# A list scheduler that waits longer for urgent work: up to 1.2 lengths of an operation instead of 0.5, in the front of a transformer block

## The chip, the cores and the metric

The kernel runs on one core of a Trainium2 chip. The metric is the device time of one execution in microseconds (us). Executions of one kernel agree within about 0.3%. All runs here were with a granted TensorE clock of 0.999 or 1.000. The profile's "span", from first to last instruction, is 1.7 to 1.8 us shorter than the time of the same execution. Engines: PE is TensorE (PEld its weight loads), DVE is VectorE, ACT is ScalarE, POOL is GpSimd, SP is the engine that issues most transfers.

## The reference

A pre-normalised block: linear attention with 32 heads and the feature map `phi`, then a gated feed-forward part, each added to its input. Sequence 2048, width 1024, inner width 3584, bf16 inputs.

```python
def _A_ref(x, wqkv, wo):                      # linear attention
    q, k, v = split_heads(x @ wqkv)           # cut
    pq, pk = phi(q), phi(k)                   # t + 1 for t > 0, else exp(t); + 1e-6
    kv = einsum("bhsd,bhse->bhde", pk, v);  z = sum of pk over s
    o = (pq @ kv) / (pq @ z + 1e-6)
    return merge_heads(o) @ wo
def _B_ref(x, W_gate, W_up, W_down):
    gate = x @ W_gate;  up = x @ W_up
    return (relu(gate) * up) @ W_down
h   = x + _A_ref(layernorm(x), wqkv, wo)
out = h + _B_ref(layernorm(h), W_gate, W_up, W_down)
```

## The kernel before

The large products use a seven-product scheme: sums and differences of blocks are formed on VectorE ("sums" in what follows), seven products are taken in place of eight, and their outputs are combined. The kernel's body does not issue instructions. It hands them to a `Plan`, which records what each reads and writes, gives each a length by a formula, and then fixes the order on every engine by simulating one schedule when the kernel is built. The order is all that survives: on the chip each engine executes its list, and semaphores make it wait.

The length formulas (`hold` is how long the engine is taken, `lat` what follows until others see the result, `acc` a surcharge for an accumulated output, `psum` whether an input lies in PSUM):

```python
if eng == "vector":
    narrow = all(self.nbytes(a) == 2 and a.space != PSUM for a in (out, *ins) if self.free(a) > 1)
    mode = {"tensor_tensor": 2, "tensor_scalar": 4, "memset": 2}.get(op, 1) if narrow else 1
    ...                                                    # cut
    return n / (0.96 * mode) + 69 + acc, 95 + self.SEM
if eng == "scalar":
    return n / 1.2 + (51 if psum else 93) + 2 * acc, 105 + self.SEM
return n * 1.15 + 100, 60 + self.SEM                       # GpSimd
```

The choice at each step (`late` is the time by which an operation should start if TensorE is not to wait, `ready` when its inputs are there, `s` the plan's clock on this engine, `a` the candidates whose predecessors are placed):

```python
now = [i for i in a if nodes[i].ready <= s]
i = min(now, key=lambda i: (nodes[i].nom if e == "tensor" else nodes[i].late, i))
v = nodes[i]
if e != "tensor":
    soon = [j for j in a if s < nodes[j].ready < s + 0.5 * v.hold and nodes[j].late < v.late - 1500.0]
    if soon:                                   # let the engine idle for the more urgent one
        i = min(soon, key=lambda j: (nodes[j].late, j))
        v = nodes[i]
        s = v.ready
v.start = s
clock[e] = s + v.hold
```

`Tile_.norm` applies the second normalisation to a tile on GpSimd, reading and writing 1024 bf16 elements per partition; a transposing transfer follows and feeds the gate stage. `Norm.finish` does the same for most tiles of the first normalisation; those are the GpSimd steps before 80 us.

Of the kernel before, what the change touches and what calls it, by code (L numbers as in the profile page):

```python
# [32 lines left out]
class Plan:  # L33
# [6 lines left out]
    WINDOW = 6000.0  # L40
    AHEAD = 120000.0
    OPENING = 45000.0

    class Node:
        __slots__ = ("eng", "calls", "preds", "hold", "lat", "open", "dma", "late", "ready", "left", "start", "nom")
# [155 lines left out]
    def schedule(self):  # L201
        nodes = self.nodes
        succs = self.order()
        engines = ("tensor", "vector", "scalar", "gpsimd", "sync")
        avail = {e: [] for e in engines}
        clock = {e: 0.0 for e in engines}
        for i, v in enumerate(nodes):
            v.left, v.ready = len(v.preds), max(0.0, v.late - self.AHEAD) if v.dma else 0.0
            if v.eng != "tensor" and v.late > 2.0 * self.OPENING:

                v.ready = max(v.ready, self.OPENING)
            if not v.left:
                avail[v.eng].append(i)
        pe = [i for i, v in enumerate(nodes) if v.eng == "tensor"]
        done, first, wire, out = set(), 0, 0.0, []
        while True:
            best = None
            for e in engines:
                a = avail[e]
                if not a:  # L220
                    continue
                if e == "sync":
                    for i in a:
                        v = nodes[i]
                        if v.late - max(clock[e], v.ready) > 6000.0:
                            v.ready = max(v.ready, wire - 2000.0)
                if e == "tensor":
                    while first < len(pe) and pe[first] in done:
                        first += 1
                    limit = nodes[pe[first]].nom + self.WINDOW  # L230
                    a = [i for i in a if nodes[i].nom <= limit]
                    if not a:
                        continue
                s = max(clock[e], min(nodes[i].ready for i in a))
                if best is None or s < best[0]:
                    best = (s, e, a)
            if best is None:
                break
            s, e, a = best
            now = [i for i in a if nodes[i].ready <= s]  # L240
            i = min(now, key=lambda i: (nodes[i].nom if e == "tensor" else nodes[i].late, i))
            v = nodes[i]
            if e != "tensor":

                soon = [j for j in a if s < nodes[j].ready < s + 0.5 * v.hold and nodes[j].late < v.late - 1500.0]
                if soon:
                    i = min(soon, key=lambda j: (nodes[j].late, j))
                    v = nodes[i]
# [3 lines that stand above are left out]
            end = s + v.hold + v.lat  # L252
            if v.dma:
                wire = max(wire, s + v.hold) + v.dma
                end = wire + v.lat - v.dma + min(4000.0, max(0.0, 0.25 * (v.late - s)))
            elif e == "sync":

                end = max(end, min(wire + 800.0, end + 2500.0))
            avail[e].remove(i)
            done.add(i)  # L260
            out.append(i)
            for j in succs[i]:
                w = nodes[j]
                r = clock[e] if w.eng == e else end
                w.ready = max(w.ready, r)
                w.left -= 1
                if not w.left:
                    avail[w.eng].append(j)
        assert len(out) == len(nodes)
        self.span = max(clock.values())  # L270
        return out
# [1303 lines left out]
```

## Time and profile before

| kernel before | us |
|---|---|
| median of 3 runs (lowest, highest) | 727.81 (727.63, 728.01) |
| span of the profiled execution | 724.3 |
| TensorE busy | 714.4 |
| stalls between matmuls, whole kernel | 10.2 |

The last row is what the distance between two matmul starts has over the usual one (215.9, 109.2 or 57.5 ns after 512, 256 or 132 columns; the prediction says why). Some profiles lack matmul records, but none lacks weight-load records, and each weight load starts 1 to 2 ns after the matmul before it. In the experiments I therefore took the starts from the weight loads and the widths from the program.

```profile
L122 DVE TENSOR_TENSOR mem<-mem 128x1024 f16<-128x1024 bf16 x10 | 6.8, 692 | 0.0
```

### The profile page before, as it was taken

What the parts mean: (1) busy time and instruction counts of PE and PEld (TensorE: products, weight loads), DVE (VectorE), ACT (ScalarE), POOL (GpSimd) and SP (SyncE); (2) the same over time, 40 slices, a digit from 0 to 9 for tenths busy, and PEclk for the clock granted to TensorE, in tenths of its full rate; (3) what the DMA queues carried; (4) which work ended last, traced back from release to release, by engine and by line L of the source; (5) the groups of instructions that cost most, each with busy time, mean ns of one, the idle gap of its engine ahead of it and who ended that gap; (6) DMA issues with size and microseconds to landing.
All of it is one profiled execution on the core that took longest, in us unless ns stands there. A gap on an engine that the chain in (4) does not pass through costs nothing.

```text
span 724.3 us, 11221 instructions
## 1 busy us (share of the span) xinstructions
PE 714.4 (99%) x4163; PEld 396.7 (55%) x4163; DVE 563.9 (78%) x954; ACT 277.3 (38%) x540; POOL 77.8 (11%) x88
## 2 busy tenths in 40 slices
PE   8999999999999999999999999999999999999998
PEld 4444545444444444444444444444444688888887
DVE  7897745887796885666767968769758879899996
ACT  5877555666554443333333333333333220001100
POOL 1342000002202110000000000000000004001452
PEclk9999999999999999999999999999999999999999
DMA  9556406069766630446145575685681878777974
GB/s 300 165 117 110 138 0 212 23 109 216 160 156 151 140 73 6 129 136 186 60 139 188 165 244 157 202 253 186 198 262 51 276 265 209 216 265 238 242 80 60
DMA packets 156503, 117.40 MB, mean 162 GB/s; under 512 B 54944, under 2 KB 140192, under 8 KB 156320
## 3 DMA queue, kind: packets, MB, share of 16 engines
q1 hardware_dynamic: 148832, 113.01, 53.9%
q0 software_dynamic: 7616, 3.67, 4.8%
q8 instruction: 32, 0.52, 0.3%
q14 instruction: 23, 0.19, 0.1%
HBM read 70.52 MB, written 34.08 MB: 144 GB/s over the span
## 4 chain that ended last, share of the span: by engine, by line
PE 85%; DVE 2%; DMA 2%; ACT 1%; issue 0%; POOL 0%; ACTq 0%
PE psum L122 85%; DVE mem L122 2%; DMA mem<-mem 2%; ACT mem L122 1%; POOL mem L122 0%; ACT tiny L122 0%; DVE tiny L122 0%; ACTq L122 0%
## 5 line engine op out<-in xcount | busy, mean ns | idle before, releaser
L122 PE MATMUL psum<-mem 128*128 128x512 f16 (+4 forms) x4147 | 713.3, 334 | 6.5 <-ACT mem L122 2.7
L122 PEld LDWEIGHTS <-mem 128*128 128x128 f16 (+1 forms) x4163 | 396.7, 98 | 323.8 <-issue 8.0
L122 DVE TENSOR_TENSOR mem<-psum,mem 128x512 f32<-128x512 f32 (+2 forms) x240 | 187.4, 794 | 99.3 <-ACT mem L122 65.1
L122 DVE TENSOR_TENSOR mem<-mem 128x512 f16<-128x512 bf16 (+8 forms) x400 | 241.6, 643 | 14.9 <-DMA mem<-mem 9.6
L122 ACT COPY mem<-psum 128x512 f32<-128x512 f32 (+2 forms) x124 | 92.7, 749 | 209.4 <-PE psum L122 197.9
L122 ACT COPY psum<-psum 128x512 f32<-128x512 f32 (+1 forms) x68 | 49.1, 722 | 160.3 <-PE psum L122 147.6
L122 POOL DMA_DIRECT2D out_dram<-mem x28 | 34.1, 1299 | 413.8 <-DVE mem L122 413.7
L122 ACT ACTIVATE mem<-psum 128x512 bf16<-128x512 f32 x90 | 53.6, 598 | 18.5 <-PE psum L122 18.0
L122 DVE SCALAR_TENSOR_TENSOR mem<-mem 128x512 bf16<-128x512 bf16 (+1 forms) x71 | 57.7, 813 | 1.3
L122 POOL TENSOR_SCALAR mem<-mem,tiny 128x1024 bf16<-128x1024 bf16 x28 | 37.5, 1338 | 196.9 <-ACT tiny L122 176.8
L122 DVE SCALAR_TENSOR_TENSOR mem<-psum,mem 128x512 bf16<-128x512 f32 x66 | 45.4, 688 | 11.9 <-PE psum L122 7.9
L122 ACT ACTIVATE mem<-mem,tiny 128x1024 bf16<-128x1024 bf16 x24 | 27.4, 1143 | 11.0 <-DVE tiny L122 5.8
L122 DVE TENSOR_SCALAR mem<-mem 128x512 bf16<-128x512 bf16 (+1 forms) x49 | 16.3, 332 | 17.6 <-ACT mem L122 17.4
L122 DVE TENSOR_TENSOR mem<-psum,tiny 128x384 bf16<-128x384 f32 (+1 forms) x48 | 22.9, 508 | 5.3 <-ACT tiny L122 3.9
L122 ACT ACTIVATE mem<-mem 128x1024 bf16<-128x1024 f32 (+1 forms) x23 | 24.3, 1056 | 6.5 <-DVE mem L122 6.4
L122 ACT ACTIVATE tiny<-tiny 128x1 f32<-128x1 f32 (+2 forms) x112 | 22.8, 206 | 7.5 <-DVE tiny L122 4.7
L122 ACT ACTIVATE tiny<-psum 128x12 f32<-128x12 f32 (+1 forms) x48 | 8.1, 169 | 13.9 <-PE psum L122 13.4
L122 DVE BATCH_NORM_STATS2 tiny<-mem 128x6 f32<-128x512 bf16 x16 | 10.2, 682 | 2.5 <-DMA mem<-in_A_x_dram 2.5
L122 ACT CAST mem<-psum 128x512 bf16<-128x512 f32 x18 | 10.4, 582 | 4.2 <-PE psum L122 3.7
L122 POOL TENSOR_SCALAR tiny<-tiny 128x1 f32<-128x1 f32 x14 | 4.7, 337 | 25.2 <-ACT mem L122 13.3
L122 ACT ACTIVATION_READ_ACCUMULATOR mem<-mem,tiny 128x1 f32 x24 | 4.5, 188 | 0.0
L122 DVE TENSOR_SCALAR tiny<-tiny 128x1 f32<-128x1 f32 x16 | 3.4, 210 | 0.3
(18 smaller groups left out, 14.4 us busy)
## 6 DMA issues: line engine op xcount, KB each, us to landing
l_dram<-mem SPq DMA_DIRECT2D x98, 128.0 KB, 2.2
mem<-l_dram SPq DMA_DIRECT2D x12, 896.0 KB, 6.4
mem<-in_A_x_dram SPq DMA_DIRECT2D x32, 256.0 KB, 3.0
mem<-in_B_W_up_dram SPq DMA_DIRECT2D x14, 512.0 KB, 5.3
mem<-in_B_W_gate_dram SPq DMA_DIRECT2D x14, 512.0 KB, 4.3
mem<-in_B_W_down_dram SPq DMA_DIRECT2D x28, 256.0 KB, 3.4
r_dram<-mem SPq DMA_DIRECT2D x56, 128.0 KB, 1.8
mem<-r_dram SPq DMA_DIRECT2D x8, 896.0 KB, 5.0
```

Source lines behind the costliest of these rows:

```text
L122: call = lambda: getattr(getattr(self.nc, eng), op)(*args, **k)
```

## The change

Its intent: while the plan's clock is below 215 us, that is up to the gate and up stage, an engine may idle for up to 1.2 lengths of the operation that it would otherwise start, if a more urgent one becomes ready in that time.

```diff
+    SHORT = 215000.0
...
-                soon = [j for j in a if s < nodes[j].ready < s + 0.5 * v.hold and nodes[j].late < v.late - 1500.0]
+                wait = (1.2 if s < self.SHORT else 0.5) * v.hold
+                soon = [j for j in a if s < nodes[j].ready < s + wait and nodes[j].late < v.late - 1500.0]
```

## The prediction

> **What bounds the kernel now.** I read the page first for engine totals, then busy time in stretches, then the chain that ended last, then what TensorE waited for, and last the timeline around its largest stalls.
>
> ```profile
> span 724.3 us, 11221 instructions
> PE 714.4 (99%) x4163; PEld 396.7 (55%) x4163; DVE 563.9 (78%) x954; ACT 277.3 (38%) x540; POOL 77.8 (11%) x88
> ```
>
> TensorE is busy for 714.4 of 724.3 us, at full granted clock, so all idle time it has is 9.9 us. The busy share alone does not prove it well fed, because a record of 379 ns covers a matmul that starts every 216 ns. I therefore also took the starts of consecutive matmuls from the trace. In the dense stretches a 512-column matmul follows the last after 215.9 ns, a 256-column one after 109 ns, a 132-column one after 57.5 ns. Whatever a gap has beyond that is a stall.
>
> The stretches show where stalls lie (columns: stretch; its length, then busy us and instructions of each engine):
>
> ```profile
> 0.00:45.00 45.00, 42.49 (x209) 19.51 (x210) 35.47 (x65) 32.16 (x71) 13.16 (x32) 1.00 0.74 207
> 45.00:100.00 55.00, 54.22 (x297) 26.24 (x296) 40.98 (x76) 36.41 (x70) 10.72 (x13) 1.00 0.45 104
> 100.00:215.00 115.00, 111.83 (x616) 54.48 (x615) 87.77 (x181) 66.36 (x167) 10.07 (x8) 1.00 0.58 136
> 215.00:400.00 185.00, 185.00 (x883) 84.94 (x882) 129.60 (x229) 70.15 (x136) 9.81 (x8) 1.00 0.45 120
> ...
> 660.00:725.00 65.00, 60.82 (x558) 54.27 (x555) 57.25 (x75) 4.97 (x9) 24.23 (x20) 1.00 0.68 140
> ```
>
> From 215 us on TensorE is full until the tail, which is the last matmul's drain, a DVE add and a store, and has nothing to do with the order of the front. The chain says the same in one line, start and length first:
>
> ```profile
> 208.32 512.51 PE psum L122 x3082
> ```
>
> So only the first 208 us can be shortened. Its stalls by my gap count after 12 us (before that it is start-up loads) are: 0.70 us at 27.8, 0.12 and 0.22 at 41, 0.73 at 54.1, 0.25 and 0.23 at 68, 0.22 at 76, 0.31 at 127.6, 0.21 and 0.18 at 146, 0.94 and 0.03 at 150, 1.62 at 191.1, 0.72 at 201.7, and 0.28, 0.09 and 0.23 at 205 to 208. Sum **7.1 us**. That is the ceiling of any gain: 1.0% of 727.8. What TensorE's stalls are put down to (total us, times, longest):
>
> ```profile
> PE psum L122 <- ACT mem L122: 2.7, 3, 1.5
> PE psum L122 <- DVE mem L122: 1.1, 2, 0.6
> PE psum L122 <- DMA mem<-mem: 0.8, 1, 0.8
> ```
>
> These sums are below 7.1 because the records of the last matmul before a gap run on into it. The largest stall has this timeline (start, length, instruction):
>
> ```profile
> 189.60 1.06 ACT L122 ACTIVATE mem<-mem 128x1024 bf16<-128x1024 f32 x1 [1.15 <-DVE mem L122]
> 190.56 1.14 ACT L122 ACTIVATE mem<-mem,tiny 128x1024 bf16<-128x1024 bf16 x1
> 191.60 0.19 ACT L122 ACTIVATION_READ_ACCUMULATOR mem<-mem,tiny 128x1 f32 x1
> 191.69 0.58 ACT L122 ACTIVATE mem<-psum 128x512 bf16<-128x512 f32 x1
> 192.17 0.57 ACT L122 COPY mem<-psum 128x512 f32<-128x512 f32 x1
> 192.63 0.59 ACT L122 COPY psum<-psum 128x512 f32<-128x512 f32 x1
> 192.79 1.46 PE L122 MATMUL psum<-mem 128*128 128x512 bf16 x6 [1.46 <-ACT mem L122]
> ```
>
> ScalarE began a square of the second normalisation (1.14 us and 0.19 for its accumulator) at 190.56. The copy of a product bank that TensorE needs next became ready at about 191.28 (the matmul at 190.90 plus its 0.38) and started only at 192.17, behind square and exp. This is the picture that the change wants to avoid: a long, patient operation starts just before a short, urgent one is ready.
>
> **What the Trainium skill says.** "PSUM — Partial Sum Buffer", section "Engine vs sequencer instructions", says that the queues of ScalarE, VectorE and GpSimd are strictly first in, first out, and that matmuls start and complete in program order. The trace agrees: the copy at 192.17 was ready and still stood behind the square. So the order that the plan emits is the order that the chip keeps, and a wrong hold is paid in full. "Perfetto Trace Analysis", section "Identifying the Most-Contended Engine", warns that matmul busy share is no measure of distance to the roofline and proposes the share of weight loads. Here that share is 55%, because one 98 ns load goes with each 216 ns matmul and, from 600 us on, with each 109 ns one; in this kernel the spacing of starts says more. The same page, section "Optimization Strategy", says to take the gaps of the critical engine and see what releases them; that is the list above.
>
> **The change, part by part.** No instruction is added or removed: the same 11,221 go out in another order. The plan is a list scheduler run when the kernel is built. When an engine has a ready operation v, it looks whether an operation with a deadline at least 1.5 us earlier becomes ready soon; if so, the engine idles until then and takes that first. "Soon" was 0.5 of v's planned length, and is now 1.2 of it while the plan's clock is under 215 us; later it stays 0.5. The plan's lengths, by its own cost lines: a ScalarE square of 1024 with accumulator 1024/1.2+93+170 = 1116 ns, so it waits up to 1.34 us where it waited 0.56; a 1024-wide exp from memory 946 ns (1.14 for 0.47); a VectorE 1024-wide f32 join 1136 ns (1.36 for 0.57); a bn_stats half or a 512-wide join 602 ns (0.72 for 0.30). The trace has 1146, 1056, 1223 and about 685 ns for them, so the plan is 3 to 14% short. The test also covers GpSimd and the DMA queue, not only the two engines named.
>
> How many could be affected: in the first 208 us ScalarE has 16 squares, 15 wide exps and 8 wide copies with accumulator, and VectorE 15 wide joins and 12 wide form sums; 66 long operations, each a place where the rule may fire. Short ones gain too little reach (0.1 to 0.2 us) to matter.
>
> What it can save: the stalls that stand behind such an operation. At 191.1 nearly all, 1.62 less the 0.57 us copy that TensorE must await but had partly hidden: about 1.2. At 27.8 two bn_stats halves stand before an add that TensorE needs: up to 0.7. At 201.7 a VectorE queue of join and sums precedes what TensorE awaits: perhaps 0.4. At 54.1 the copy starts as soon as its matmul group is done, so there is nothing to save, and the 0.94 at 150 waits for a transpose DMA. The dozen small ones: say 0.5 of their 2. Sum **about 2.8 us** if all fall out well.
>
> What it costs: each hold idles its engine for up to 1.3 us where it would have worked. Off the critical path this is free as long as there is slack, and there is: over 0 to 215 us VectorE is busy 164.2 of 215 us (76%), ScalarE 134.9 (63%). But the delayed square or statistics feed a normalisation, a transpose DMA and then the next stage's left sums; that chain already binds just ahead of the gate stage (around 180 to 208 us the chain is ACT, POOL, DMA, DVE by turns). I put off 0.6 us for one or two such new stalls. Net about **-2.2 us**, that is 725.6.
>
> **The rivals.** First, a wash: the plan's clock and the chip's differ by fractions of a us, so that the operation that the plan holds for is ready earlier or later on the chip. For it speaks that at 190.56 the exp's bank had been finished at about 190.42 on the chip already, so the plan's order there came from its deadlines or its own clock, and a longer hold need not touch it. Result 727 to 728.5. Second, the new order makes a longer stall: the holds delay norms, the transposes come late, and the gate stage starts later than 208 us. For it speaks the 0.94 us stall on a transpose at 150 and the thin margin in 180 to 208; against it the 24 to 37% slack. Result 728.5 to 731. Third, the holds gain almost everything, because order changes propagate and clear the 201 to 208 group as well: 721 to 723. The DMA or another engine becoming the bound is excluded: the bytes are the same, and the matmul stream from 208 us on is gapless for 512 us.
>
> **Range and chances.** I weigh the main path (-1 to -3.5 us) at 0.58, the wash at 0.22, the worse order at 0.12, the large gain at 0.08. Middle 725.6, eight in ten between 722.4 and 728.9. Faster by 2% needs 14.6 us, twice the 7.1 us that exist: 0.005. Slower by 2% needs 14.6 us of new stalls in 208 us of work: 0.015. Within 2%: 0.98.
>
> **What would show it.** Right: the long piece of TensorE work at the end of the chain keeps its length (512.5 us) and starts earlier, at about 206 instead of 208.3; the 1.62 us stall near 191 falls below 0.6; the stall near 27.8 shrinks; ScalarE shows more small idle pieces ahead of copies from PSUM, and busy totals stay. Wrong in size: the gap list after 12 us still sums to about 7, with other places. Wrong in sign: TensorE waits for transposes or for VectorE sums between 140 and 208 us, and the long piece starts after 209. Wrong in kind: any new gap after 215 us, where the rule did not change but inherits the state of a shifted plan; that would mean that order changes leak into the gate stage.

## More of the kernel before

Besides the views in the prediction two more are needed. One is the 1024-wide sums of the front, as a group (count, busy us, mean ns of one). The other is VectorE on the timeline ahead of the largest stall (start, length, instruction, and in brackets how long the engine idled before it and what ended that):

```profile
187.93 0.42 DVE L122 TENSOR_TENSOR mem<-mem 128x512 f16<-128x512 bf16 x1 [2.76 <-DMA mem<-mem]
188.27 0.68 DVE L122 SCALAR_TENSOR_TENSOR mem<-psum,mem 128x512 bf16<-128x512 f32 x1
188.88 0.08 DVE L122 DVE_READ_ACCUMULATOR mem<-psum,mem 128x1 f32 x1
188.88 0.69 DVE L122 TENSOR_TENSOR mem<-psum,mem 128x512 f32<-128x512 f32 x1
```

A sum sits at the head of VectorE's queue and waits 2.76 us for a transposing transfer. Behind it stand a join and an add that read finished products.

`GW.sums` forms four differences of gate and up weights for each group; they are needed only when the gate stage starts, so in the plan they have 47 to 56 us of slack.

## The result, and the profile after

| | median us | lowest to highest | runs |
|---|---|---|---|
| before | 727.72 | 726.88 to 728.07 | 6 |
| changed | 727.68 | 727.52 to 728.00 | 6 |

The ratio is 1.0002 (95% interval 0.9989 to 1.0015). Ratios here are the mean time of one kernel's fast runs over that of the other's in the same rounds, so not quite the ratio of the medians quoted. The change did nothing that can be measured.

The head of the changed kernel's page:

```profile
span 725.8 us, 11170 instructions
...
PE 711.1 (98%) x4112; PEld 396.6 (55%) x4163; DVE 566.4 (78%) x954; ACT 276.9 (38%) x540; POOL 80.4 (11%) x88
```

The program still has 4163 matmuls; 51 of their records are missing, as the count of weight loads shows, and with them 3 us of "busy". The busy time in stretches:

```profile
45.00:100.00 55.00, 52.77 (x287) 25.95 (x292) 41.69 (x79) 36.97 (x74) 13.99 (x15) 1.00 0.49 115
100.00:215.00 115.00, 111.66 (x601) 54.30 (x611) 89.46 (x179) 67.05 (x168) 9.87 (x8) 1.00 0.57 134
215.00:400.00 185.00, 184.16 (x872) 85.09 (x887) 129.36 (x232) 70.31 (x136) 9.82 (x8) 1.00 0.46 121
```

The 0.84 us that TensorE seems to idle in 215 to 400 are missing records (887 weight loads, 872 matmuls); by the weight loads there is no stall. In 45 to 100 us GpSimd is busy for 13.99 us where it was 10.72. What TensorE's stalls are put down to:

```profile
PE psum L123 <- DVE mem L123: 3.1, 5, 1.5
PE psum L123 <- ACT mem L123: 2.8, 3, 1.9
PE psum L123 <- DMA mem<-mem: 0.6, 1, 0.6
```

Waits for VectorE grew from 1.1 to 3.1 us; those for ScalarE stayed. So the change did not find nothing to do. It removed stalls and made others. A place-by-place account follows, in us. It has two profiles of each kernel, because the first profile of before was a fast execution (726.09) and the second (727.37) is nearer to the median; times in the heading are those of the first profile of before.

| stalls of TensorE | before | before, again | changed | changed, again |
|---|---|---|---|---|
| start, under 12 | 2.85 | 3.35 | 3.12 | 4.12 |
| 28 | 0.70 | 0.68 | 1.64 | 1.52 |
| 40 to 52 | 0.36 | 0.36 | 0.02 | 0.02 |
| 54 | 0.73 | 1.61 | 2.08 | 2.08 |
| 60 to 100 | 0.76 | 0.98 | 0.18 | 0.18 |
| 125 to 156 | 1.77 | 1.78 | 1.29 | 1.31 |
| 160 to 185 | 0.02 | 0.02 | 1.23 | 1.24 |
| 191 | 1.62 | 1.30 | 0.37 | 0.37 |
| 195 to 215 | 1.37 | 1.37 | 1.68 | 1.68 |
| sum | 10.2 | 11.4 | 11.6 | 12.5 |
| span | 724.3 | 725.6 | 725.8 | 726.7 |

Against the second profile of before, the first of the changed kernel gains 0.34 + 0.80 + 0.49 + 0.93 = 2.6 us at four places and loses 0.96 + 0.47 + 1.21 + 0.31 = 3.0 us at four others. The start varies by itself.

The loss at 160 to 185 has a shape of its own: three stalls, of 0.21, 0.50 and 0.51 us, at 166, 171 and 176. The second, on the timeline of VectorE, of GpSimd and of TensorE:

```profile
169.29 1.19 POOL L123 TENSOR_SCALAR mem<-mem,tiny 128x1024 bf16<-128x1024 bf16 x1 [4.09 <-ACT tiny L123]
...
169.87 1.15 DVE L123 TENSOR_TENSOR mem<-mem 128x1024 f16<-128x1024 bf16 x1
...
170.94 0.68 DVE L123 SCALAR_TENSOR_TENSOR mem<-psum,mem 128x512 bf16<-128x512 f32 x1
...
171.68 1.02 PE L123 MATMUL psum<-mem 128*128 128x512 bf16 x4 [0.34 <-DVE mem L123]
```

A 1024-wide sum takes 1.15 us, begins inside a GpSimd step and ends 0.54 us after it; the join behind it, for which TensorE waits, is late. As a group the sums now read

```profile
L123 DVE TENSOR_TENSOR mem<-mem 128x1024 f16<-128x1024 bf16 x8 | 6.9, 858 | 0.1
```

and the mean rose from 692 to 858 ns because three of the eight take 1.15 us and five 0.68. Those three are `GW.sums`, and in the kernel before they ran at 137.6, 138.3 and 143.7 us. In the changed plan the longer hold passed them over again and again: something more urgent was always due within 0.72 us (1.2 of their planned 0.602). They came to run at 164.6, 169.9 and 175.2.

The Trainium skill has the mechanism. "SBUF — State Buffer", section "Who interferes with whom", says that VectorE and GpSimd share one pair of ports to the memory under an exclusive lock, that "A DVE instruction with two SBUF inputs contends with a GpSimd instruction that reads SBUF", and that the loser blocks until the other is through. The trace agrees: in all three cases the sum ends 0.54 or 0.55 us after the GpSimd step.

The gain at 191 is on VectorE too. The same place in the changed kernel:

```profile
188.51 0.69 DVE L123 SCALAR_TENSOR_TENSOR mem<-psum,mem 128x512 bf16<-128x512 f32 x1 [0.36 <-PE psum L123]
...
189.37 0.69 DVE L123 TENSOR_TENSOR mem<-psum,mem 128x512 f32<-128x512 f32 x1
189.98 1.54 DVE L123 TENSOR_TENSOR mem<-mem 128x512 f16<-128x512 bf16 x4
```

Join and add now come first, and the sum that waits for the transfer comes after them. In the plan the join was due 0.18 us after the sum; half of the sum's planned length of 0.336 us is 0.168, so the old rule missed it by some 0.01 us, and 1.2 lengths caught it. ScalarE's order around 191 (copy, wide exp, square, exp, copy) is the same in both kernels.

The largest stall of the changed kernel, 2.08 us at 54, shows the same meeting from GpSimd's side (ScalarE, GpSimd and TensorE):

```profile
50.06 4.38 POOL L123 TENSOR_SCALAR mem<-mem,tiny 128x1024 bf16<-128x1024 bf16 x2
...
54.65 1.15 ACT L123 ACTIVATE mem<-mem,tiny 128x1024 bf16<-128x1024 bf16 x1 [1.94 <-POOL tiny L123]
...
57.23 1.02 PE L123 MATMUL psum<-mem 128*128 128x512 f16 x4 [1.92 <-ACT mem L123]
```

The two GpSimd steps take 2.53 and 1.85 us, where others take 1.19; four of VectorE's two-input sums run beside them. ScalarE has a square at the head of its queue that waits 1.94 us for GpSimd, and behind it stand the copies that TensorE needs. This is read from the trace; no run tested it alone.

### The profile page after: what moved, and what is told of

It is laid out like the page before. It is cut to its first block, busy times and chain, and to the rows that moved or that the text cites. A ratio compares the mean times of both kernels' runs of the same rounds, so it can differ in the third digit from the quotient of the medians.

```text
span 725.8 us, 11170 instructions
## 1 busy us (share of the span) xinstructions
PE 711.1 (98%) x4112; PEld 396.6 (55%) x4163; DVE 566.4 (78%) x954; ACT 276.9 (38%) x540; POOL 80.4 (11%) x88
## 4 chain that ended last, share of the span: by engine, by line
PE 88%; ACT 2%; DMA 1%; issue 1%; DVE 1%; POOL 0%; DVEq 0%; ACTq 0%
PE psum L123 88%; ACT mem L123 1%; DVE mem L123 1%; DMA mem<-in_B_W_up_dram 1%; DMA mem<-mem 0%; ACT tiny L123 0%; DVE tiny L123 0%; POOL tiny L123 0%; DVEq L123 0%; ACTq L123 0%
## 5 line engine op out<-in xcount | busy, mean ns | idle before, releaser
L123 PE MATMUL psum<-mem 128*128 128x512 bf16 (+4 forms) x4096 | 710.0, 334 | 11.1 <-DVE mem L123 3.1
L123 POOL TENSOR_SCALAR mem<-mem,tiny 128x1024 bf16<-128x1024 bf16 x28 | 39.7, 1417 | 182.3 <-ACT tiny L123 168.9
L123 DVE SCALAR_TENSOR_TENSOR mem<-psum,mem 128x512 bf16<-128x512 f32 x66 | 45.2, 687 | 10.2 <-PE psum L123 6.3
```

What stands on the lines that cost most here:

```text
L123: call = lambda: getattr(getattr(self.nc, eng), op)(*args, **k)
```

## The experiments

Theory: the gains and the losses are both real, and the largest loss comes from sums that the hold pushed beside GpSimd's steps. Rivals: (a) elastic: the chain of normalisations sets when the product near 191 may start, so any stall before it is only moved; (b) run-to-run timing of transfers decides; (c) a full VectorE queue, not GpSimd, makes the stalls at 166 to 176.

Medians of before were 727.27, 727.44 and 727.63 us (9 runs each). All results were correct. Edits are against the changed kernel's line `wait = ...` unless said.

**The two kernels again.** No edit.

> The kernel before, unchanged, for a second profile. If TensorE's stalls follow from the order (theory), the list after 12 us repeats: 7.1 to 7.5 us in sum, with 1.62 near 191, 0.70 near 27.8 and 0.73 near 54.1, each within 0.1. If run-to-run timing of transfers decides (rival), single stalls differ by 0.5 us or more and the span lies up to 1.7 us above the 724.3 of the first profile.

> The changed kernel, unchanged, for a second profile. Theory of cancelling: the same stalls again, about 1.6 at 28, 2.1 at 55, 0.2 + 0.5 + 0.5 at 166, 171 and 176, 0.4 at 193.5, sum 8.5; ratio 0.999 to 1.001. Rival (run-to-run timing): the stalls at 28 and 55 move by 0.5 us or more between the two profiles.

Before: 727.38 us, 0.9999 (0.9985 to 1.0013). Changed: 727.97, 1.0004 (0.9990 to 1.0017). The table above has the stalls. Most repeat within 0.1 us. In before those at 54 (0.73 and 1.61), at 191 (1.62 and 1.30) and at 76 (0.22 and 0.44) do not, nor does the start; the first two were expected to. In both profiles of before one 512-wide sum just ahead of the stall at 54 begins 0.17 us after the record of a GpSimd step. In the faster one the sum took 0.42 us and GpSimd's step 1.48; in the slower the sum took 1.30 and the step 1.19. In four of the five profiles with the order of before up to there, the stall is 1.61. Rival (b) holds for the start and for 54, for a third of a microsecond at 191, and not for the rest.

**The far sums stay where they were.** "Far" means more than 35 us of slack; over such an operation the old 0.5 stays.

```diff
+wait = (1.2 if s < self.SHORT and v.late - s < 35000.0 else 0.5) * v.hold
```

> The longer hold, except over operations with more than 35 us of slack, so the gate weights' sums stay near 138 to 155 us. Theory: the three sums take 0.69 us instead of 1.15, the stalls at 166, 171 and 176 (1.22 us in sum) go, and TensorE passes 192 us and the span ends 1.2 us earlier than in the changed kernel, ratio about 0.998 against before. Rival (elastic): the chain of normalisations sets the start of the product near 193 anyway, the wait there grows by 1.2 us and the span stays as in the changed kernel.

726.98 us, 0.9995 (0.9983 to 1.0008); span 725.2. The four sums run at 139.9 to 157.2 us and take 0.68 each, and the stalls at 160 to 185 are 0.02 in sum. At 191 the stall is 0.37 as in the changed kernel, so nothing was moved there: against (a). 0.78 us came back at 125 to 156, so the net against the changed kernel is about 0.6 us by the span and 1.0 by the medians, less than the 1.2 expected.

**One engine alone.**

```diff
+wait = (1.2 if s < self.SHORT and e == 'vector' else 0.5) * v.hold    # VectorE alone
+wait = (1.2 if s < self.SHORT and e == 'scalar' else 0.5) * v.hold    # ScalarE alone
```

> The longer hold for VectorE alone. If ScalarE's holds caused the longer stall at 55 us (they postpone a square that then stands behind a late GpSimd step), that stall is back at 0.7 us and the span is 1.3 us shorter than the changed kernel's; the 166 to 176 stalls stay at 1.2. If VectorE's holds caused it by slowing GpSimd, it stays at about 2. The 1.62 us stall of before at 191 stays gone if VectorE's hold over the sum that waits for the transpose removed it, and comes back if ScalarE's hold over the square did.

> Longer hold for ScalarE alone. Theory: no stalls at 166 to 176 (the sums stay), the 191 stall stays at 1.3 to 1.6 because VectorE's order there is as before, and the stall at 55 is 1.4 to 2.1, as long as in the changed kernel; ratio 1.000 to 1.002. If ScalarE's holds are what gains (as predicted), the 191 stall falls below 0.6 here and the ratio is under 0.999.

VectorE alone: 726.48 us, 0.9987 (0.9974 to 0.9999). The 191 stall is gone (0.00), those at 166 to 176 are there (1.23), the places around 54 sum to 1.07 (neither the 0.7 nor the 2 of the expectation), and 195 to 215 costs 2.07 where before had 1.37. ScalarE alone: 726.75 us, 0.9990 (0.9978 to 1.0003), where 1.000 to 1.002 was expected. The 191 stall is 1.44, no stalls at 160 to 185 (0.02), 54 at 1.44; it gains at 60 to 100 (0.08). So VectorE's holds cured 191 and made 166 to 176. The prediction had given 191 to ScalarE.

**VectorE alone, far sums stay; and both engines from 100 us on, far sums stay.**

```diff
+wait = (1.2 if s < self.SHORT and e == 'vector' and v.late - s < 35000.0 else 0.5) * v.hold
+wait = (1.2 if 100000.0 <= s < self.SHORT and v.late - s < 35000.0 else 0.5) * v.hold
```

> Longer hold for VectorE alone and never over operations with more than 35 us of slack. Theory (gains are real, losses are the collisions of VectorE with GpSimd): the 166, 171 and 176 stalls (1.22 us) of the VectorE-only version go, the rest stays; span 1.2 us under that version, ratio about 0.997 against before. Rival (elastic): the time stays at the VectorE-only version's 0.9987.

> Longer hold for both engines only from 100 us of the plan on, and never over operations with more than 35 us of slack. Theory: up to 100 us the order is that of before, so stalls to there are as in the two profiles of before (1.0 in 12 to 45, 1.5 to 2.6 in 45 to 100); none at 166 to 176; 191 at 0.4 instead of 1.3 to 1.6; span about 1.0 us under before, ratio 0.998 to 0.999.

The first: 726.77 us, 0.9990 (0.9976 to 1.0003), not the 0.997 expected. The 166 to 176 stalls went (0.02), but 125 to 156 cost 1.79 instead of 1.02, 191 0.57 instead of 0.00, and in the profiled execution 54 cost 2.00 instead of 1.07. The second: 727.43, 0.9996 (0.9984 to 1.0009). Its stalls came as expected (0.02 at 160 to 185, 0.37 at 191), but 195 to 215 cost 0.32 more than before and 125 to 156 0.3 more, so of 0.93 gained at 191 some 0.3 is left, and the timed runs do not show even that.

**Only the sums moved, into and out of GpSimd's way.** Both are the kernel before, with a line ahead of the scheduling loop that makes these operations ready no earlier than a given time. The first uses the 0.88 us slots that overlap a GpSimd step, as the changed plan did; the second uses 1.45 us slots of the same stage in which GpSimd rests.

```diff
+for i, at in ((545, 166400.0), (548, 171450.0), (554, 176500.0)): nodes[i].ready = at
+for i, at in ((545, 163950.0), (548, 169000.0), (554, 174050.0), (557, 179100.0)): nodes[i].ready = at
```

> The kernel before with one thing altered: three of the gate weights' sums may not start before 166.4, 171.45 and 176.5 us of the plan, as in the changed kernel, where each has a slot of 0.88 us beside a GpSimd step. Theory (shared access to memory): they take about 1.15 us instead of 0.69, end some 0.55 us after GpSimd's step, and TensorE loses 0.2 + 0.5 + 0.5 us near 166, 171 and 176. Rival (elastic): the same stalls, but the one at 191 shrinks by as much.

> As the last, but the sums are put in the same busy stage at 163.95, 169.0, 174.05 and 179.1 us of the plan, where GpSimd rests. Theory: they take 0.69 us each and TensorE loses nothing there (under 0.1). Rival (a full VectorE queue, not GpSimd, makes the stalls): stalls of 0.2 to 0.5 us at three of these places too.

Beside GpSimd: 729.47 us, 1.0026 (1.0012 to 1.0040), slower than before beyond the noise. The three sums take 1.15 us, TensorE loses 0.22, 0.51 and 0.51 us at 167, 172 and 177, and the stall at 191 did not shrink but grew to 2.08. The fourth sum followed by itself, to 173.9 us, clear of GpSimd, and took 0.68. Clear of GpSimd: 727.38 us, 0.9997 (0.9983 to 1.0011), sums of 0.68 us, no stall over 0.04 at 160 to 185, 191 at 1.35. That settles (a). Against (c) speaks that the lost time lies inside the sum's own record (1.15 instead of 0.68); but the slots of the two runs also differ in width, so the second run alone does not exclude a fuller queue. The timeline with the sums beside GpSimd:

```profile
165.23 1.20 POOL L122 TENSOR_SCALAR mem<-mem,tiny 128x1024 bf16<-128x1024 bf16 x1 [3.33 <-ACT tiny L122]
...
165.81 1.15 DVE L122 TENSOR_TENSOR mem<-mem 128x1024 f16<-128x1024 bf16 x1
...
166.89 0.68 DVE L122 SCALAR_TENSOR_TENSOR mem<-psum,mem 128x512 bf16<-128x512 f32 x1
```

and clear of it:

```profile
164.36 1.20 POOL L122 TENSOR_SCALAR mem<-mem,tiny 128x1024 bf16<-128x1024 bf16 x1 [3.33 <-ACT tiny L122]
...
167.22 0.68 DVE L122 TENSOR_TENSOR mem<-mem 128x1024 f16<-128x1024 bf16 x1
...
167.82 0.69 DVE L122 TENSOR_TENSOR mem<-psum,mem 128x512 f32<-128x512 f32 x1
```

The reader is to compare the 1024-wide sum of each: the same instruction type, in the same stage, 0.47 us longer where the GpSimd step covers its start.

**A plan that knows of the shared access.** A flag marks VectorE sums with both inputs in memory and GpSimd steps of 512 elements or more. A flagged operation starts no earlier than the end of the other engine's last flagged one, and VectorE prefers other ready work meanwhile.

```diff
+held = {"vector": 0.0, "gpsimd": 0.0}
...
+if e == "vector" and s < held["gpsimd"]:
+    now = [i for i in now if not nodes[i].pair] or now
...
+if v.pair:
+    s = max(s, held["vector" if e == "gpsimd" else "gpsimd"])
+    held[e] = s + v.hold
```

It was run with three hold rules: that of before (0.5); 1.2 for both engines with far sums staying; 1.2 for VectorE alone with far sums staying.

> The order rule of before (0.5), but the plan knows that VectorE's two-input sums and GpSimd steps never run side by side. Theory of two gains: the stall at 55 is under 0.5 us in place of 0.7 to 1.6, the 191 stall stays at 1.3 to 1.6; ratio about 0.9985. If this knowledge alone made the best version, it gets 0.997.

> The longer hold for both engines, not over operations with more than 35 us of slack, with the same knowledge of GpSimd. Theory: the 28 and 55 stalls fall below 1.1 and 0.5 us, 166 to 176 none, 191 at 0.4; ratio 0.996 to 0.998. If ScalarE's holds harm by themselves, the stall at 55 stays over 1.4 us and the ratio is 0.998 to 1.000.

> As the VectorE-only version without far operations, and the plan also knows that a VectorE operation with two inputs in memory and a GpSimd operation never run side by side, and lets VectorE take other work meanwhile. Theory: VectorE's two-input sums that overlap GpSimd fall from about ten in the changed kernel to two or less, their mean is under 0.02 us above the undisturbed one, and the stalls at 28 and 55 fall below 1.0 each; ratio 0.996 to 0.998. Rival: the plan's clock is too far off to avoid them, and it equals the version without this knowledge.

With the rule of before: 727.25 us, 0.9998 (0.9985 to 1.0012); the stall at 54 stays at 1.61, so what I expected of the knowledge alone did not come. With both engines: 726.90, 0.9992 (0.9979 to 1.0004); 54 at 2.05, which is the branch of the expectation in which ScalarE's holds harm. With VectorE alone: **725.32 us** against 727.44, 0.9970 (0.9957 to 0.9982), the largest gain (VectorE alone, at 0.9974 to 0.9999, is only just clear of before); 160 to 185 at 0.02, 191 at 0.37, and 54 at 0.24. Its five runs (724.69 to 725.63) all lie below the five of the version without the knowledge (726.39 to 727.85). Of its gain the cure at 191 is understood. Why 54 clears with this combination and not with either half is not: I saw it in one profile. There the two GpSimd steps at 52.9 and 54.8 us take 1.19 us each and no square waits for GpSimd; but ten of VectorE's two-input sums of the front still lie beside a GpSimd step, not two as expected; two of them are lengthened, by 0.9 us together, and the stall at 28 is 1.06. The plan's clock differs from the chip's by up to 4.0 us in the front (the product at 165.0 us was planned for 168.5 in before), so a plan can only make such meetings less likely.

## Why the prediction was right or wrong

- **The bound and the ceiling** were right. From 208 us on TensorE had nothing to gain; past the last stall of the front, at 211.7, the lag between the two first profiles stays at 1.43 us to the end. No new stall appeared after 215. The rule could only move the front's 7 us of stalls, and 2% was out of reach.
- **The time** was inside the range, 2.1 us above the point, but that is owed to the range's width: the main path, -1 to -3.5 us, missed, and the time fell where the rival of a wash had put it. The step that failed is "Net about **-2.2 us**". Its cost of "0.6 us for one or two such new stalls" was mis-sized: the losses measured 3.0 us. Its gain of 2.8 was about right in sum (2.6 measured), but by luck, since it came from other places than named.
- **What it costs** was looked for in the wrong place. I priced the idle time of the holding engine and the delay of square and statistics. The largest single loss, 1.2 us, came from operations with about 50 us of slack, which were passed over until they met GpSimd. I did not ask where the passed-over work would land. Moving just these sums cost 0.26% of the time (1.0026), of which 1.2 us at the sums and the rest mostly at 191, and moving them clear of GpSimd cost nothing.
- **The 191 stall**: "nearly all ... about 1.2" was right in size, 1.62 to 0.37 between the first profiles (0.93 against the second). Its cause was wrong. It was not the square on ScalarE, whose order there did not change; with ScalarE's holds alone the stall stayed at 1.44. All seven versions with VectorE's longer hold in that stage have 0.00 to 0.57, all five without it 1.24 to 2.08. That the one hold over the sum that waits for a transfer does it is what the traces show; no run undid it alone.
- **"Short ones gain too little reach (0.1 to 0.2 us) to matter"** was wrong: that hold is 0.18 us long, over a sum of 0.336.
- **27.8**, "up to 0.7" saved, went the other way, 0.68 to 1.64. Versions with VectorE's longer hold there have 1.05 to 1.64, those without 0.61 to 0.73. In both profiles of the changed kernel a 2048-wide sum ahead of it takes 2.06 us instead of 1.22 beside GpSimd. **201.7** kept its stall. **54.1**, "nothing to save", lost 0.5 against the usual 1.61. With both engines' holds (1.73 to 2.08) ScalarE's square waits 1.6 to 1.9 us for GpSimd each time, as shown above; with one engine's the wait is absent (1.07 and 2.00 with VectorE's, 1.44 with ScalarE's), and what makes 2.00 stays open. The small ones at 40 to 52, 60 to 100 and 125 to 156 gave 1.6 us (0.34 + 0.80 + 0.49), not 0.5.
- **The rivals**: the wash came true in size only. Its reason, a plan clock that misses, was not tested by itself; what the runs show is that the holds did act, 52 of them longer than the old rule allows (41 on VectorE, 10 on ScalarE, 1 on the transfer queue, counted in the plan), and gains and losses cancelled. The late transposes of the second rival did not show; the stall before the transposed tile at 150 fell from 0.94 to 0.75.
- **The signs it named**: the stall near 191 fell below 0.6, but the one near 27.8 grew, and the long piece of TensorE work starts at 212.5 us, not at 206 (the last stall of the front now lies later in the stream). TensorE also waited for VectorE sums between 140 and 208 us. These last two are its signs of "wrong in sign", although the time stayed the same; the list after 12 us sums to 8.4 to 8.5 us, against 7.3 and 8.1 before.

## What to carry to other kernels

When a scheduler may idle for urgent work, ask where the passed-over work will run, not only what the wait costs: operations with much slack are passed over until they land in the fullest stage. Exempting them took the stalls there from 1.23 to 0.02 us, though other places took part of it back. If two engines share an access to memory, put that into the plan's model and measure it together with the thresholds: here the knowledge paid with one of three hold rules (0.9970, against 0.9998 and 0.9992). A zero in the total can be the sum of 2.6 gained and 3.0 lost, which a place-by-place list of the critical engine's stalls shows and a share of busy time does not.

## What the Trainium skill lacked or had wrong

- "SBUF — State Buffer" has the lock, but not how it looks in a profile. Here the wait lies inside the blocked VectorE record: the 1024-wide sum reads 1.15 us instead of 0.68, and ends 0.54 us after GpSimd's step; GpSimd's step at 50 us reads 2.53 instead of 1.19.
- "Perfetto Trace Analysis" proposes weight-load share over matmul share; that page does not say that matmul records can be missing. Here one profile has 4112 of 4163 and another of the same length all 4163, while weight loads were complete in both. The share itself, 55% in both kernels, did not help; the spacing of weight-load starts gave every stall to about 0.01 us.
- "SBUF — State Buffer", in the same section, says that issue order decides who blocks. The order of the records does not tell which that is: with one order a sum that began 0.17 us after GpSimd's record took 0.42 us in one execution (GpSimd 1.48) and 1.30 in another (GpSimd 1.19), and TensorE's stall behind it was 0.73 and 1.61 us.
